# Attention scores for the row maxima as two half-height products, norms merged by pairs of heads, casts moved to ScalarE

## The chip, the cores and the metric

One core of a Trainium2 chip runs the whole program in one launch. The metric is the device time of the program in microseconds; smaller is better. The engines named in the profile are PE (TensorE, its matmuls), PEld (its weight loads), DVE (VectorE), ACT (ScalarE), POOL (GpSimd) and SP (SyncE, which issues most DMAs).

## The reference

The program is an attention block, a routing of tokens to experts and two feed-forward layers. Only the first part is touched by the change. It has B = 4, H = 8, S = 576 and D = 64:

```python
scores = scale * np.matmul(q, k.transpose(0, 1, 3, 2))
scores = np.where(causal, -1000000000.0, scores)
scores = scores - scores.max(-1, keepdims=True)
a = np.exp(scores)
a /= a.sum(-1, keepdims=True) + 1e-09
local = np.matmul(a, v)
...
q_p = phi(q)
mem_ret = np.einsum('bhsd,bhde->bhse', q_p, M_prev)
mem_norm = np.einsum('bhsd,bhd->bhs', q_p, z_prev)[..., None] + 1e-06
mem_out = mem_ret / mem_norm
return (g * mem_out + (1 - g) * local).astype(np.float32)
```

After it each token goes to one of 8 experts by a greedy pass over all gate values with a capacity of 288, through `relu(x @ w1) @ w2` of its expert, and through `max(x @ w1, x @ w2, x @ w3) @ w_out`.

## The kernel before

The heads are worked on in 16 pairs. The scores of a head are computed twice. The first time rows of q are the partitions (`s`, line L509 for the four full blocks of 128 rows, L511 for the last 64 rows of both heads), and VectorE takes each row's maximum from PSUM (L528, an operation and a read of its accumulator). The maxima are turned by a product with the identity (L562), copied by ScalarE and written by a small DMA into an extra row of `QL`. The second time keys are the partitions (`t`, L629 and L630, four groups for each head), with the maximum already subtracted by that extra row; ScalarE takes the exponential into `PT` (L640), GpSimd cuts the triangle off (L658), and fifteen products with V for each head (`av`, L675) add up the output and the row sum. The norm (L693, L696, L700, L704, all on VectorE) divides and adds to `x`, which already holds the memory part (`mem`, L724; L748).

Precision comes from splitting float32 into two float32r parts. `Kr` and `Qr` hold each head's 64 rows of k and q twice, in partitions 0 to 63 and 64 to 127. `QX` is the rounded q in both halves; `KX` is the rounded k in both halves, from which the lower half is then replaced by the rest k - KX. One product over 128 partitions therefore gives q times (rounded k + rest). `KB` and `QL` carry the other rest. The three casts of a head (`KX`, `QX`, `KB`, all recorded at the helper line L312) may go to ScalarE or VectorE, whichever a planner finds sooner free; the rests (recorded at L84) go to GpSimd. The products with V and those of L724 and L407 are plain float32 and appear as two records each.

What sets the order: every piece of work is a task with a key, a cost for each engine and the ring of buffers that it needs. `Plan.run` simulates the engines with those costs and writes all instructions out in the order in which it started them. Keys and costs of `PRIO`, `act`, `dve` and the numbers at each `add` thus set the order on all five engines; each engine runs its list strictly in order. The rings that matter here are `s` with 3 PSUM banks, `t` with 2, `av` with 2 (one for each head of a pair) and `mem` with 1. To keep PSUM for the fourth, 64-wide score group of a head, that group is written into unused columns of the head's `av` bank:

```python
bt = Buf(R["t"]) if gi < 3 else r.bav[i]
```

While the first data is loading, TensorE runs 32 products of a constant (`warm`, L790) in pairs over 64 partitions each; their result is not used. 24 conversions of the second layer's weights (L869 on ScalarE, L873, L876, L879 on VectorE) fill gaps of the attention. The attention ends when the last gate values are in `L`; then the routing begins on VectorE and TensorE.

Of the kernel before, what the change touches and what calls it, by code (L numbers as in the profile page):

```python
# [22 lines left out]
F32 = mybir.dt.float32  # L23
# [32 lines left out]
BUFS = {'Kr': 2, 'Qr': 2, 'QN': 2, 'MZ': 2, 'V': 3, 'VT': 2, 'phi': 2, 'ph': 1, 'KX': 6, 'QX': 5, 'QL': 2, 'KB': 4, 'QJ': 3, 'nm': 3, 'nmr': 1, 'n9': 1, 'PT': 2, 's': 3, 't': 2, 'r5': 2, 'tmp': 3, 'rm': 2, 'x': 2, 'm2raw': 2, 'm2a': 1, 'm2b': 1, 'x2': 2}  # L56
OFFK = (0, 576, 1024, 1344, 1536)
ACTX = 0
PRIO = {'load': -12, 'phi': 2.0, 'min2': ['ACT'], 'prep': 7.5, 'cpe': ['ACT', 'DVE'], 'sube': ['POOL'], 'S': -71.0, 'J4': -2.0, 'R': -78.0, 'E': 29.0, 'N': -37.5, 'T': -3.0, 'A': 18.5, 'M': -60.0, 'rowe': ['ACT'], 'maske': ['POOL'], 'norm': 0.5, 'xadd': ['DVE'], 'mem': [0, 9], 'gate': 45.5, 'G': -13.0, 'gev': ['ACT'], 'm2': [15.0, 4.6, 25.0]}
# [7 lines left out]
NROW, COLD, NLAT = 1, 6000, 3000  # L67
# [64 lines left out]
class Plan:  # L132
# [28 lines left out]
    def run(self):  # L161
# [7 lines left out]
        while len(order) < len(self.tasks):  # L169
            best, hold, cands = None, {}, []  # L170
            for t in ready:
                blocked, users = False, []
                for b in t.new:
                    k = len(b.ring.made) - b.ring.n
                    if k >= 0:
                        users += b.ring.made[k].users
                if any(u.end is None for u in users) or not all(b.made for b in t.use):
                    continue
                for e, c in t.engs.items():
                    if e == "PE" and now < self.cold:  # L180
                        c *= 2
                    at = 0
                    for d in t.deps:
                        at = max(at, d.end + (LAT[d.eng][e] + d.slack * (d.eng != e) if d.lat is None else d.lat))
                    for u in users:
                        at = max(at, u.end + (0 if u.eng == e else LAT[u.eng][e]))
                    st = max(at, free.get(e, 0), now)
                    cands.append((t, e, c, st))
# [57 lines left out]
def attention(g, tc, ctx, consts, beta, qT, kT, qN, v1, vT, mz, mT, wg, xd, L, m2):  # L246
# [20 lines left out]
    AV = [ps.tile([128, 512], F32, name=f"av{i}") for i in range(2)]  # L267
# [4 lines left out]

    def av3(t):
        return t[:, :NJ * C].rearrange("p (j c) -> p j c", j=NJ)
# [30 lines left out]
    def act(n, psum=False):  # L305
        return 22 + 0.89 * n if psum else 60 + 0.89 * n
# [37 lines left out]
    def pair(p):  # L344
# [92 lines left out]
        r.tphi = add(kp + .2, {"DVE": dve(S)}, phi3, [a], use=[b_["ph"], b_["phi"], b_["QN"]])  # L437
# [10 lines left out]
        def head(i):  # L448
# [13 lines left out]
            def sk(e):  # L462
                sub(nc, e, r.KX[i][64:], r.Kr[64:, i], r.KX[i][64:].bitcast(F32))
# [12 lines left out]
            sb = {x: {"POOL": 1390, "DVE": dve(S)}[x] for x in W["sube"]}  # L476
            if not p:
                cp, sb = {"ACT": act(S), "DVE": dve(S, False)}, {"POOL": 1390, "DVE": dve(S)}
# [12 lines left out]
    def maxes(r, p):  # L491
# [5 lines left out]
        def piece(key, heads, j, a, z, first, last, dep):  # L497
# [6 lines left out]
            for x, i in enumerate(heads):  # L504
                def fS(e, i=i, x=x):
                    if x == 0:
                        o.s = ps.tile([128, 512], F32, name="s", bufs=BUFS["s"])
                    if j < 4:
                        nc.tensor.matmul(o.s[:, :z - a], r.QX[i][:, 128 * j:128 * j + 128], r.KX[i][:, a:z], start=True, stop=True)  # L509
                    else:  # L510
                        nc.tensor.matmul(o.s[:, :z - a], u.QJ[:, i], r.KX[i][:, a:z], start=x == 0, stop=x == len(heads) - 1)  # L511

                ts.append(add(key + 5 * heads[-1] + W["S"], {"PE": mm(z - a)}, fS, r.th[i] + ts[-1:] + u.prev + (tj[i:i + 1] if j == 4 else []),
                              new=[bs] if x == 0 else [],
                              use=[r.bh[i]["KX"], r.bh[i]["QX"]] + [bs] * x + ([bj] if j == 4 else [])))

            def fR(e):
# [15 lines left out]
            ttr.append(add(key + 5 * heads[-1] + W["R"], {"DVE": max(dve(z - a), 196)}, fR, ts + dep, new=[bnm] if new else [],  # L533
# [12 lines left out]
        each = []  # L546
        for i in range(2):
            e0 = len(ttr)
            for j in range(4):
                piece(n + j, (i,), j, 0, 128 * j + 128, True, True, ttr[-1:])  # L550
            if p < NROW:
                t = piece(n + 4, (i,), 4, 0, 512, True, False, ttr[-1:])
                piece(n + 4, (i,), 4, 512, S, False, True, t)
            each.append(ttr[e0:])
# [49 lines left out]
    def unit(r, p, i):  # L604
# [14 lines left out]
        for gi, gr in enumerate(groups):  # L619
            o = K()  # L620
            bt = Buf(R["t"]) if gi < 3 else r.bav[i]

            def fT(e, gr=gr, o=o, gi=gi):
                o.t = ps.tile([128, 512], F32, name="t", bufs=BUFS["t"]) if gi < 3 else AV[h % 2][:, 448:512]
# [23 lines left out]
        for gi, (kb, cnt, st) in enumerate(((0, 2, 576), (2, 2, 320), (4, 1, 64))):  # L648
# [12 lines left out]
            c = {"DVE": dve(cnt * m), "POOL": 40 + 1.25 * cnt * m}  # L661
# [3 lines left out]
        for j in range(NJ):  # L665
            m = rows(j)

            def fA(e, j=j, m=m):

                av = AV[h % 2][:, j * C:j * C + CA]  # L670
                for kb in range(j + 1):
# [3 lines left out]
                    nc.tensor.matmul(av[:m], u.PT[:kr, o:o + m], r.Vw[:kr, c:c + CA],  # L675
                                     start=(kb == 0), stop=(kb == j))

            out.append(add(n1 + W["A"] + .1 * j, {"PE": (222, 444, 666, 888, 700)[j]}, fA,
                           mk[:1] + (fill if p == 0 else []) + (ex[1:2] if j else []) + (mk[1:2] if j > 1 else []) + (mk[2:] if j > 3 else []) + [r.tV] + out[-1:],
                           use=[bP, r.b["V"], r.bav[i]]))  # L680
        return out

    def norm(r, p, i, deps, mems):
        b, pp = divmod(p, H // 2)
        h = 2 * pp + i
        n = r.n + 5 * i + 4 + W["norm"]
        av = av3(AV[h % 2])
# [3 lines left out]
        def f1(e):  # L691
            u.r5 = tile("r5", [128, NJ])
            V.tensor_scalar(u.r5, av[:, :, 72], 1.0e-9, g.c1[:, h:h + 1], op0=OP.add, op1=OP.mult)  # L693
# [4 lines left out]
        def f3(e):  # L698
            u.tmp = tile("tmp", [128, NJ, 72])
            V.tensor_mul(u.tmp, av[:, :, :72], u.r5[:, :, None].to_broadcast([128, NJ, 72]))  # L700

        def f4(e):
            for x, c0, c1 in ((x2s[b].t[:, :, h], 0, 64), (xs[b][:, :, h], 64, 72)):
                vg(e).tensor_add(x, x, u.tmp[:, :, c0:c1])  # L704

        t = add(n, {"DVE": 130}, f1, deps + [cdone], new=[br], use=[r.bav[i]])
        t = add(n + .1, {"DVE": 100}, f2, [t], use=[br])
        t = add(n + .2, {"DVE": dve(360)}, f3, [t], new=[bt], use=[br, r.bav[i]])
        c = {"POOL": 1020, "DVE": dve(320) + 90}
        return add(n + .3, {x: c[x] for x in (W["xadd"] if p < NP - 1 else ("POOL", "DVE"))}, f4, [t] + mems, use=[bt, r.bx, r.bx2])  # L710

    def mem(r, p, part):
# [39 lines left out]
        t = add(n + .1, {"DVE": 75}, f1, [t, cdone], new=[br], use=[bm])  # L752
        t = add(n + .2, {"DVE": 80}, f2, [t], use=[br])
        return add(n + .3, {"DVE": dve(144 * k) + 70}, f3, [t] + ([firsts[b]] if b in firsts else []),
# [67 lines left out]
    for p in range(NP):  # L822
# [24 lines left out]
    def conv(k):  # L847
# [36 lines left out]
        t2 = add(n + W["m2"][2], {"DVE": 335}, f2, [t0], new=[bb], use=[br])  # L884
        t3 = add(n + W["m2"][2] + .1, {"DVE": 602}, f3, [t1, t2], use=[ba, bb])
        add(n + W["m2"][2] + .2, {"DVE": 602}, f4, [t3], use=[br, bb])
# [689 lines left out]
```

## Time and profile before

| | us |
|---|---|
| median of three runs | 941.97 (934.69, 941.97, 942.91) |
| the profiled execution's own time | 938.56 |
| its span, first to last instruction | 936.8 |
| TensorE busy | 863.9 (92%) |
| VectorE busy | 570.9 (61%) |
| GpSimd busy | 433.6 (46%) |
| ScalarE busy | 316.5 (34%) |

Shares over the whole span mix stages. The attention fills the first 297 us or so, the routing of the first expert some 60 us after it, and the experts the rest. A matmul's end is modelled, so that a TensorE that shows as busy can still be slowed by weight loads; how far apart two products start says more than how long each is shown. A float32 product is two records.

### The profile page before, as it was taken

To read this page: it belongs to the slowest core of one execution; us is meant where nothing else is said; L and a number is where in the kernel's file an instruction comes from. 1 tells how busy PE (TensorE), PEld (TensorE's weight loads), DVE (VectorE), ACT (ScalarE), POOL (GpSimd) and SP (SyncE) were. 2 spreads that over 40 slices of the span, in tenths; PEclk is the share of its full clock that TensorE was granted. 3 is DMA by queue.
4 is the path that set the end of the run, shared out by engine and by line. 5 is a ranking of instruction groups with operands and counts; after the bars stand their busy time and mean duration, and the time that the engine had idled before them with its cause. 6 is when DMAs were issued, how large, how long until landed. Compare 5 with 4: busy or idle time off the path is not lost.

```text
span 936.8 us, 17494 instructions
## 1 busy us (share of the span) xinstructions
PE 863.9 (92%) x6493; PEld 788.0 (84%) x6493; DVE 570.9 (61%) x1708; ACT 316.5 (34%) x683; POOL 433.6 (46%) x665
## 2 busy tenths in 40 slices
PE   8999999999997467999989998999999999979997
PEld 5888888888886357989979988989998998979996
DVE  5699999997756864842682683484376386123121
ACT  3445555553334032223124133224223224322211
POOL 1758777677421396344064155136208326730301
PEclk9699999999998569999999999999999999989999
DMA  7456776854201122231042032024014114340000
GB/s 282 164 200 201 252 256 218 281 162 133 94 18 52 54 62 91 72 112 46 2 138 91 2 115 95 21 79 138 23 47 146 38 52 154 116 91 23 24 1 34
DMA packets 37601, 97.86 MB, mean 104 GB/s; under 512 B 9620, under 2 KB 9740, under 8 KB 37516
## 3 DMA queue, kind: packets, MB, share of 16 engines
q1 hardware_dynamic: 34240, 87.24, 28.8%
q0 software_dynamic: 2976, 9.44, 3.0%
q8 instruction: 51, 0.84, 0.4%
q14 instruction: 34, 0.28, 0.1%
q10 hardware_dynamic: 300, 0.07, 0.0%
HBM read 87.22 MB, written 9.45 MB: 103 GB/s over the span
## 4 chain that ended last, share of the span: by engine, by line
PE 61%; DVE 11%; POOL 10%; issue 8%; DMA 8%; ACT 2%; SPq 0%; POOLq 0%; ACTq 0%; DVEq 0%
PE av L675 10%; PE w L1323 7%; PE w L1325 7%; PE w L1324 7%; DMA wraw<-in_wr 5%; PE acc L1325 4%; PE acc L1323 4%; PE acc L1324 4%; POOL ml L84 4%; POOL wlo L84 3%; PE s L509 3%; PE t L629 2%; PE mem L724 2%; PE t L630 2%; PE mem L407 2%
## 5 line engine op out<-in xcount | busy, mean ns | idle before, releaser
L84 POOL TENSOR_TENSOR wlo<-wraw,whi 128x256 fp32r<-128x256 f32 x224 | 167.6, 783 | 253.2 <-ACT whi L1289 251.1
L1323 PE MATMUL w<-yh,mh 128*128 128x288 f32 x576 | 175.1, 304 | 4.8 <-ACT mt L1425 4.8
L1324 PE MATMUL w<-yl,mh 128*128 128x288 f32 x576 | 171.7, 298 | 0.1
L1325 PE MATMUL w<-yh,ml 128*128 128x288 f32 x576 | 171.1, 297 | 0.0
L675 PE MATMUL av<-V,PT 128*128 128x112 f32 (+2 forms) x960 | 130.7, 275 | 0.0
L675 PEld LDWEIGHTS av<-V,PT 128*128 128x128 f32 (+2 forms) x960 | 114.9, 174 | 13.7 <-issue 4.6
L1323 PEld LDWEIGHTS w<-yh,mh 128*128 128x128 f32 x576 | 109.9, 191 | 8.0 <-ACT mt L1425 5.0
L1324 PEld LDWEIGHTS w<-yl,mh 128*128 128x128 f32 x576 | 109.9, 191 | 3.4 <-DVE yl L1229 0.3
L1325 PEld LDWEIGHTS w<-yh,ml 128*128 128x128 f32 x576 | 110.1, 191 | 0.0
L1227 DVE SCALAR_TENSOR_TENSOR hl<-w,hh 128x288 fp32r<-128x288 f32 x64 | 28.8, 456 | 132.3 <-ACT hh L1221 132.3
L1427 DVE TENSOR_TENSOR mt<-w,mt 128x288 f32<-128x288 f32 x96 | 43.5, 453 | 102.9 <-PE w L1325 84.0
L1289 ACT CAST whi<-wraw 128x1024 fp32r<-128x1024 f32 x64 | 67.2, 1049 | 114.9 <-DMA wraw<-in_wr 89.9
L528 DVE CUSTOM_DVE_ANT_0 junk<-s,mask 128x256 bf16<-128x256 f32 (+4 forms) x145 | 72.8, 505 | 23.6 <-PE s L509 19.8
L1325 PE MATMUL w<-xhi,wlo 128*128 128x288 f32 x256 | 77.7, 304 | 8.1 <-DVE wlo L78 7.5
L640 ACT ACTIVATE PT<-t 128x512 f32<-128x512 f32 x96 | 54.5, 594 | 78.7 <-PE av L675 48.7
L1323 PE MATMUL w<-xhi,whi 128*128 128x288 f32 x256 | 78.0, 305 | 1.1 <-ACT whi L1289 1.1
L1324 PE MATMUL acc<-hl,whi 128*128 128x288 f32 x256 | 76.8, 300 | 0.8 <-DVE hl L1227 0.8
L1324 PE MATMUL w<-xlo,whi 128*128 128x288 f32 x256 | 77.1, 301 | 0.0
L1323 PE MATMUL acc<-hh,whi 128*128 128x288 f32 x256 | 77.1, 301 | 0.0
L1325 PE MATMUL acc<-hh,wlo 128*128 128x288 f32 x256 | 76.5, 299 | 0.0
L84 POOL TENSOR_TENSOR KX<-Kr,KX 64x192 fp32r<-64x192 f32 x90 | 63.1, 729 | 21.0 <-ACT KX L312 13.8
L658 POOL TENSOR_SCALAR_AFFINE_SELECT PT<-PT 128x256 f32<-128x256 f32 (+1 forms) x96 | 41.2, 440 | 66.7 <-ACT PT L640 61.2
(236 smaller groups left out, 1925.0 us busy)
## 6 DMA issues: line engine op xcount, KB each, us to landing
wraw<-in_wr SPq DMA_DIRECT2D x64, 512.0 KB
Kr<-in_kT SPq DMA_DIRECT2D x15, 576.0 KB
Qr<-in_qT SPq DMA_DIRECT2D x15, 576.0 KB
V<-in_v SPq DMA_DIRECT2D x16, 384.5 KB
m2raw<-in_m2w SPq DMA_DIRECT2D x12, 512.0 KB
QN<-in_qN SPq DMA_DIRECT2D x16, 288.0 KB
VT<-in_vT SPq DMA_DIRECT2D x16, 288.0 KB
xd<-x SPq DMA_DIRECT2D x16, 256.0 KB
```

The costliest lines, as they stand in the source:

```text
L84: u = nc.gpsimd.tensor_sub(o[:, c], a[:, c], b[:, c])
L509: nc.tensor.matmul(o.s[:, :z - a], r.QX[i][:, 128 * j:128 * j + 128], r.KX[i][:, a:z], start=True, stop=True)
L528: V.tensor_tensor_reduce(out=junk[ps_, :z - a], in0=o.s[ps_, :z - a], in1=mask[ps_, k:k + z - a], scale=-0.125, scalar=init, op0=OP.add, o ...
L640: A.activation(u.PT[:kr, at0:at0 + wd], o.t[:kr, :wd], AF.Exp, scale=0.125)
L658: G.affine_select(v, v, pattern=[[1, m]] if cnt == 1 else [[0, 2], [1, m]], compare_op=OP.is_ge, fill=0.0, base=0, channel_multiplier=-1)
L675: nc.tensor.matmul(av[:m], u.PT[:kr, o:o + m], r.Vw[:kr, c:c + CA], start=(kb == 0), stop=(kb == j))
L1227: V.scalar_tensor_tensor(lo(), src(), 0.0, hi().bitcast(F32), op0=OP.max, op1=OP.subtract)
L1289: A.copy(x.W[fb][0], x.RAW[fb])
L1323: nc.tensor.matmul(o, wh, rh, start=start, stop=False)
L1324: nc.tensor.matmul(o, wh, rl, start=False, stop=False)
L1325: nc.tensor.matmul(o, wl, rh, start=False, stop=stop)
L1427: V.tensor_max(q.mt, o.pt[:, :T], q.mt)
```

## The change

1. `fS` for the four full blocks: both heads' products are issued back to back, head 0 from partitions 0 to 63 of `KX` and `QX`, head 1 from partitions 64 to 127, each into its own bank of `s`. They use the rounded k alone. For that `sk` writes head 1's rest into the upper half of `KX`, so that its rounded k stays in the lower one. The reductions (`reduce`, split off from `piece`) stay one for each head and block. The last 64 rows (L511) are as before.
2. `norm` is called once for a pair, over both `av` banks, which are now one tile `AVP`. A head's first product with V therefore takes a bank that the norm of the whole pair before releases. The last block's product with V writes 73 columns in place of 112.
3. The 64-wide score group goes into a bank of the `t` ring.
4. `cpe` is ScalarE alone, but for the first pair.
5. Keys and costs of the planner are other numbers, its check of free buffers counts two new buffers of one ring in one task, and it doubles TensorE's costs in its first 25,000 ns in place of 6,000. `xadd` is on VectorE for the last pair too.

```diff
-BUFS = {... 'tmp': 3, ...}
+BUFS = {... 'tmp': 2, ...}
...
-PRIO = {'load': -12, 'phi': 2.0, ... 'cpe': ['ACT', 'DVE'], 'sube': ['POOL'], 'S': -71.0, 'J4': -2.0, 'R': -78.0, 'E': 29.0, 'N': -37.5, 'T': -3.0, 'A': 18.5, 'M': -60.0, ... 'norm': 0.5, ...}
+PRIO = {'load': -22, 'phi': -18.0, ... 'cpe': ['ACT'], 'sube': ['POOL'], 'S': -51.0, 'J4': -2.0, 'R': -96.0, 'E': 29.0, 'N': -47.5, 'T': -41.0, 'A': 40.5, 'M': 10.0, ... 'norm': -9.5, ...}
...
-NROW, COLD, NLAT = 1, 6000, 3000
+NROW, COLD, NLAT = 1, 25000, 3000
...
-    AV = [ps.tile([128, 512], F32, name=f"av{i}") for i in range(2)]
+    AVP = ps.tile([128, 2, 512], F32, name="av")
+    AV = [AVP[:, i] for i in range(2)]
...
     def act(n, psum=False):
-        return 22 + 0.89 * n if psum else 60 + 0.89 * n
+        return 135 + 0.89 * n if psum else 155 + 0.89 * n
...
             def sk(e):
-                sub(nc, e, r.KX[i][64:], r.Kr[64:, i], r.KX[i][64:].bitcast(F32))
+                q = slice(64 - 64 * i, 128 - 64 * i)
+                sub(nc, e, r.KX[i][q], r.Kr[q, i], r.KX[i][q].bitcast(F32))
...
-        each = []
+
+        each = [[], []]
+        for j in range(4):
+            bs = [Buf(R["s"]) for _ in range(2)]
+            os = [K(), K()]
+            z = 128 * j + 128
+
+            def fS(e, j=j, z=z, os=os):
+                for i in range(2):
+                    os[i].s = ps.tile([128, 512], F32, name="s", bufs=BUFS["s"])
+                for i in range(2):
+                    q = slice(64 * i, 64 * i + 64)
+                    nc.tensor.matmul(os[i].s[:, :z], r.QX[i][q, 128 * j:z], r.KX[i][q, :z], start=True, stop=True)
+
+            t = add(n + j + W["S"], {"PE": mm(z) + 60}, fS, r.th[0][:2] + r.th[1][:2] + u.prev, new=bs,
+                    use=[r.bh[i][x] for i in range(2) for x in ("KX", "QX")])
+            for i in range(2):
+                each[i] += reduce(n + j + .5 * i, (i,), j, 0, z, True, True, ttr[-1:], os[i], slice(0, 128), bs[i], [t])
         for i in range(2):
-            e0 = len(ttr)
-            for j in range(4):
-                piece(n + j, (i,), j, 0, 128 * j + 128, True, True, ttr[-1:])
...
-            bt = Buf(R["t"]) if gi < 3 else r.bav[i]
+            bt = Buf(R["t"])
...
-                av = AV[h % 2][:, j * C:j * C + CA]
+                w = CA if j < 4 else C
+                av = AV[h % 2][:, j * C:j * C + w]
...
-    def norm(r, p, i, deps, mems):
+    def norm(r, p, deps, mems):
...
         def f3(e):
-            u.tmp = tile("tmp", [128, NJ, 72])
-            V.tensor_mul(u.tmp, av[:, :, :72], u.r5[:, :, None].to_broadcast([128, NJ, 72]))
+            u.tmp = tile("tmp", [128, NJ, 2, 72])
+            V.tensor_mul(u.tmp, av[:, :, :, :72], u.r5[:, :, :, None].to_broadcast([128, NJ, 2, 72]))
...
-        for i in range(2):
-            last = unit(r, p, i)
-            nm.append(norm(r, p, i, last, [m0, m1]))
+        last = unit(r, p, 0) + unit(r, p, 1)
+        r.avs = [r.bav[0], r.bav[1]]
+        nm.append(norm(r, p, last, [m0, m1]))
```

**The order on TensorE.** Before, in the second and third pair, the score products for the maxima (`s<-KX,QX`) stand one by one between products with V (`av`) and the gate's products (`mem<-wb,VT`); the next head's products with V follow on the other bank.

```order
L675 MATMUL av_109<-V,PT 128x112 x4
L509 MATMUL s<-KX,QX 128x128 [waits DVE_49,Pool_49]
L675 MATMUL av_109<-V,PT 64x112 x5
L509 MATMUL s<-KX,QX 128x256 [waits DVE_49,Pool_49]
L407 MATMUL mem<-wb,VT 128x96 [waits DMAHW4_49,DVE_49]
L407 MATMUL mem<-wb,VT 128x96 x3
L407 MATMUL mem<-wb,VT 64x96
L509 MATMUL s<-KX,QX 128x384
L675 MATMUL av_110<-V,PT 128x112
L509 MATMUL s<-KX,QX 128x512 [waits DVE_49,Pool_49]
```

After, at the boundary between the third and the fourth pair, they stand in twos (`x2`, or two rows where the second waits for something else), and the new pair's first product with V, the last row, waits for VectorE (the norm of the pair before) and GpSimd.

```order
L557 MATMUL s<-KX,QX 128x128 [waits DVE_49] x2
L574 MATMUL s<-ident,nm 9x128 [waits DVE_49]
L641 MATMUL t<-QX,KX 128x320 [waits Activation_49]
L642 MATMUL t<-QL,KB_127 128x320
L641 MATMUL t<-QX,KX 128x192
L642 MATMUL t<-QL,KB_127 128x192
L405 MATMUL mem<-wb,VT 128x96 [waits DVE_49]
L405 MATMUL mem<-wb,VT 128x96 x3
L405 MATMUL mem<-wb,VT 64x96
L641 MATMUL t<-QX,KX 64x64 [waits Activation_49]
L642 MATMUL t<-QL,KB_127 64x64
L557 MATMUL s<-KX,QX 128x256 [waits DVE_49]
L557 MATMUL s<-KX,QX 128x256 [waits Activation_49]
L688 MATMUL av<-V,PT 128x112 [waits DVE_49,Pool_49]
```

In all, the score products for the maxima moved together by twos, and the `t` groups of the next heads stand between the last product with V of a pair and the first of the next.

**The order on VectorE.** Before, in the first pair, head 0's norm begins with `r<-av,c` and releases the bank with `tmp<-av,r`; a row maximum, a cast, a reciprocal and a weight conversion stand between.

```order
L693 TENSOR_SCALAR r_596<-av_109,c_120 128x5 [waits PE_49]
L528 ISA junk,nm<-s,mask 128x256 [waits DVE_49,PE_49]
L528 ISA nm 128x1
L312 CAST KX<-Kr 128x576 [waits DMAHW7_49]
L696 RECIPROCAL r_596<-r_596 128x5 [waits DVE_49]
L876 SCALAR_TENSOR_TENSOR m2b<-m2a,m2b 128x512 [waits Activation_49]
L700 TENSOR_TENSOR tmp<-av_109,r_596 128x360 [waits DVE_49]
```

After, the norm at the boundary between the third and the fourth pair: the same two ends, over 10 and 720 elements, and between them the memory part's `x<-mem,rm` and two row maxima.

```order
L707 SCALAR_TENSOR_TENSOR r_1130<-av,c_119 128x10 [waits PE_49]
L762 TENSOR_TENSOR x_467<-mem,rm 128x3x128 [waits DVE_49]
L762 TENSOR_TENSOR x<-mem,rm 128x3x16
L527 ISA junk,nm<-s,mask 128x128 [waits PE_49]
L527 ISA nm 128x1
L710 RECIPROCAL r_1130<-r_1130 128x10 [waits DVE_49]
L527 ISA junk,nm<-s,mask 128x128 [waits PE_49]
L527 ISA nm 128x1
L714 TENSOR_TENSOR tmp<-av,r_1130 128x720 [waits DVE_49]
```

The norms of two heads became one, the cast of `KX` left this engine, and row maxima that wait for TensorE still stand inside the norm.

## Rows read from the trace of the kernel before

**Rows 1.** Busy time by engine in stretches (microseconds, instructions), granted clock, DMA share, GB/s

```profile
core 0: us, PE busy (x) PEld busy (x) DVE busy (x) ACT busy (x) POOL busy (x), PEclk, DMA share, GB/s
...
28.00:45.00 17.00, 16.54 (x64) 14.68 (x65) 10.70 (x39) 8.10 (x19) 13.41 (x24) 0.51 0.39 132
...
60.00:200.00 140.00, 137.44 (x1000) 119.29 (x1000) 134.31 (x430) 75.13 (x160) 106.14 (x161) 1.00 0.72 236
200.00:280.00 80.00, 76.67 (x562) 66.78 (x562) 57.07 (x196) 31.98 (x69) 41.66 (x110) 1.00 0.29 91
...
```

**Rows 2.** Waits of TensorE from 60 to 280 us, longest in total first

```profile
PE s L562 <- DVE nm L528: 3.4, 4, 1.0
...
```

**Rows 3.** Timeline of TensorE's products, 240.2 to 243.1 us: start, duration, instruction

```profile
240.29 0.42 PE L509 MATMUL s<-KX,QX 128*128 128x384 f32 x1
240.65 1.31 PE L675 MATMUL av<-V,PT 128*64 128x112 f32 x10
241.89 0.50 PE L509 MATMUL s<-KX,QX 128*128 128x512 f32 x1
242.23 0.37 PE L675 MATMUL av<-V,PT 128*128 128x112 f32 x2
242.37 0.48 PE L511 MATMUL s<-KX,qj 128*128 128x512 f32 x1
242.68 0.59 PE L675 MATMUL av<-V,PT 128*128 128x112 f32 x4
```

**Rows 4.** Timeline of TensorE's products, 2 to 12.4 us

```profile
2.48 3.00 PE L790 MATMUL av<-warm 64*128 64x384 f32 x16 [2.48 <-DVE av L270]
...
7.47 0.58 PE L509 MATMUL s<-KX,QX 128*128 128x256 f32 x1
7.98 0.69 PE L790 MATMUL av<-warm 64*128 64x384 f32 x2
8.60 0.69 PE L509 MATMUL s<-KX,QX 128*128 128x384 f32 x1
...
```

**Rows 5.** Timeline of TensorE's products, 233 to 252 us, 64-wide scores

```profile
236.40 0.19 PE L629 MATMUL av<-QX,KX 128*64 128x64 f32 x1
236.44 0.22 PE L630 MATMUL av<-QL,KB 65*64 65x64 f32 x1
236.49 0.90 PE L675 MATMUL av<-V,PT 128*128 128x112 f32 x6
```

**Rows 6.** Groups of VectorE by form, 0 to 305 us: busy us, mean ns | idle before

```profile
L704 DVE TENSOR_TENSOR x<-x,tmp 128x320 f32<-128x320 f32 x32 | 21.5, 672 | 0.3
...
L700 DVE TENSOR_TENSOR tmp<-av,r 128x360 f32<-128x360 f32 x32 | 16.9, 527 | 0.4
...
L704 DVE TENSOR_TENSOR x<-x,tmp 128x40 f32<-128x40 f32 x32 | 11.6, 362 | 0.0
L312 DVE CAST KB<-Kr 64x576 fp32r<-64x576 f32 x19 | 11.3, 595 | 0.5 <-PE av L630 0.5
L528 DVE CUSTOM_DVE_ANT_0 junk<-s,mask 128x128 bf16<-128x128 f32 x32 | 9.0, 282 | 3.3 <-PE s L509 3.3
...
L312 DVE CAST QX<-Qr 128x576 fp32r<-128x576 f32 x13 | 7.1, 556 | 0.0
L693 DVE TENSOR_SCALAR r<-av,c 128x5 f32<-128x5 f32 x32 | 7.1, 221 | 15.5 <-PE av L675 13.4 <-ACT mh L1200 2.0
L696 DVE RECIPROCAL r<-r 128x5 f32<-128x5 f32 x32 | 5.9, 184 | 0.2
...
```

**Rows 7.** Groups of ScalarE by form, 0 to 305 us

```profile
L312 ACT CAST KX<-Kr 128x576 fp32r<-128x576 f32 x19 | 12.5, 662 | 0.0
...
```

**Rows 8.** Timeline of TensorE's products, 24.3 to 28.5 us

```profile
27.38 0.42 PE L590 MATMUL t<-identr,nmr 128*1 128x128 f32 x4 [1.53 <-DVE nmr L584]
```

More of the change, by code (lines that the diff above doesn't have):

```diff
@@ L171, in run @@
             for t in ready:
-                blocked, users = False, []
-                for b in t.new:
-                    k = len(b.ring.made) - b.ring.n
+                users = []
+                for y, b in enumerate(t.new):
+                    k = len(b.ring.made) - b.ring.n + sum(q.ring is b.ring for q in t.new[:y])
                     if k >= 0:
@@ L436, in pair @@
         a = add(kp + .1, {"ACT": act(S)}, phi2, [a], use=[b_["ph"]])
[L437 removed]
+        r.tphi = add(kp + .2, {"DVE": dve(S) + 140}, phi3, [a], use=[b_["ph"], b_["phi"], b_["QN"]])
         def scale(e):
@@ L507, in fS @@
                         o.s = ps.tile([128, 512], F32, name="s", bufs=BUFS["s"])
[L508 to L511, printed above, removed]
+                    nc.tensor.matmul(o.s[:, :z - a], u.QJ[:, i], r.KX[i][:, a:z], start=x == 0, stop=x == len(heads) - 1)
                 ts.append(add(key + 5 * heads[-1] + W["S"], {"PE": mm(z - a)}, fS, r.th[i] + ts[-1:] + u.prev + (tj[i:i + 1] if j == 4 else []),
@@ L515, in piece, with reduce @@
                               use=[r.bh[i]["KX"], r.bh[i]["QX"]] + [bs] * x + ([bj] if j == 4 else [])))
+            return reduce(key, heads, j, a, z, first, last, dep, o, ps_, bs, ts)
+        def reduce(key, heads, j, a, z, first, last, dep, o, ps_, bs, ts):
             def fR(e):
@@ L532, in piece @@
             new = not ttr
-            ttr.append(add(key + 5 * heads[-1] + W["R"], {"DVE": max(dve(z - a), 196)}, fR, ts + dep, new=[bnm] if new else [],
+            ttr.append(add(key + 5 * heads[-1] + W["R"], {"DVE": 235 + 1.02 * (z - a)}, fR, ts + dep, new=[bnm] if new else [],
                            use=[bs] + ([] if new else [bnm])))
@@ L620, in unit @@
             o = K()
-            bt = Buf(R["t"]) if gi < 3 else r.bav[i]
+            bt = Buf(R["t"])
             def fT(e, gr=gr, o=o, gi=gi):
-                o.t = ps.tile([128, 512], F32, name="t", bufs=BUFS["t"]) if gi < 3 else AV[h % 2][:, 448:512]
+                o.t = ps.tile([128, 512], F32, name="t", bufs=BUFS["t"])
                 c = 0
@@ L698, in f3 @@
         def f3(e):
-            u.tmp = tile("tmp", [128, NJ, 72])
-            V.tensor_mul(u.tmp, av[:, :, :72], u.r5[:, :, None].to_broadcast([128, NJ, 72]))
+            u.tmp = tile("tmp", [128, NJ, 2, 72])
+            V.tensor_mul(u.tmp, av[:, :, :, :72], u.r5[:, :, :, None].to_broadcast([128, NJ, 2, 72]))
         def f4(e):
             for x, c0, c1 in ((x2s[b].t[:, :, h], 0, 64), (xs[b][:, :, h], 64, 72)):
[L704 to L710, printed above, removed]
+                vg(e).tensor_add(x, x, u.tmp[:, :, :, c0:c1])
+        t = add(n, {"DVE": 214}, f1, deps + [cdone], new=[br], use=r.avs)
+        t = add(n + .1, {"DVE": 180}, f2, [t], use=[br])
+        t = add(n + .2, {"DVE": dve(720) + 60}, f3, [t], new=[bt], use=[br] + r.avs)
+        c = {"POOL": 2040, "DVE": 1250}
+        return add(n + .3, {x: c[x] for x in W["xadd"]}, f4, [t] + mems, use=[bt, r.bx, r.bx2])
     def mem(r, p, part):
```

43 lines of the change are left out of this document (20 added, 23 removed).

## Prediction

> **What bounds the kernel now.** I read the busy time by stretches first, then TensorE's waits, then its timeline. The attention ends near 297 us; the order behind it is unchanged, so what the change is worth is how much earlier that end comes. From 60 to 200 us TensorE is busy for 137.4 of 140 us at the full clock, VectorE for 134.3, GpSimd for 106, ScalarE for 75 [rows 1]. Two engines look full, and which one is the bound decides everything. The list of TensorE's waits answers: in 220 us it waited for VectorE in four waits of 3.4 us together that are worth naming [rows 2], and its products otherwise start at spacings that repeat. So TensorE is the bound, VectorE is merely as busy, and work taken off VectorE gives back little more than those 3.4 us. I therefore price the change on TensorE.
>
> **Prices on TensorE.** All from the timeline. A product with V over 128 columns of weights and 112 moving columns takes 0.11 us for each of its two records. A 512-column score product between two such takes 0.45 - 2 x 0.11 = 0.23 us (242.23 to 242.68) [rows 3], that is 512 columns at 2.4 GHz (0.213) and about 0.02 to 0.03 us. With 0.03 for each, the four blocks of a head are 1280 columns, 0.53 + 0.12 = 0.65 us, 1.30 for a pair.
>
> What does a product over 64 partitions cost among others over 128? At the start, with the engine at 1.2 GHz, the rows show it. Sixteen of the constant products, issued by twos over the two halves, take 3.0 us, 0.32 to 0.37 for two of 384 columns, so the two halves do run side by side (384 columns at 1.2 GHz are 0.32). But two of them alone between score products take from 7.98 to 8.60, 0.62 us, and the 256-column score product before them 0.51 where its columns take 0.21 [rows 4]: 0.30 us goes at each change between the two forms. At full clock I have the plain float32 products with 64 columns of weights, the last two of them over 64 partitions. From 240.29 to 242.23 stand a 384-column score product, ten such records and a 512-column one [rows 3]. Without changes that would be 0.19 + 10 x 0.095 + 0.24 = 1.38 (0.093 are 2 x 112 columns at 2.4 GHz); it took 1.94. Three changes cost 0.56, 0.19 each. Half of the 0.30 at half the clock is 0.15. These are the ends; I take 0.16, nearer to the lower, since a start is shown a little early behind a faster stream. The 64-wide float32r score groups pay nothing of the kind (starts 0.04 to 0.05 apart [rows 5]), so narrow weights alone are no change of form there.
>
> The Trainium skill, page TensorEngine Tiling (Array Packing), section Key Properties, says that a change of tiling mode, as against a change of tile, drains TensorE, while tiles of one mode work independently. The start rows agree on both, with 0.30 us for a change; the page gives no price.
>
> **The change part by part.**
> 1. *Score products by twos.* The columns of one of two products are saved: 0.65 us for a pair. Behind the first pair's products with V, the order holds 57 such twos: 57 x 0.163 = -9.3 us. The same order has 228 changes of form against 138 (counted over rows of half height and of narrow float32). 90 x 0.16 = +14.4 us, between +13.5 and +17. If weights could be loaded across the change, it would be 0: that is a rival.
> 2. *73 columns in place of 112.* Each of 30 blocks has ten records, 2 x 39 columns fewer at 2.4 GHz, 0.0325 us each: 0.31 us allowing for the two that follow a change. 30 x 0.31 = -9.3. It holds only if 64 columns of weights load faster than 0.06 us; three starts 0.04 and 0.05 apart say so [rows 5]. The other end is 0, if the 0.095 us are weight loading.
> 3. *Maxima and the small product that waits for them* (L562). Its wait for VectorE is 3.4 us [rows 2]. It now stands two to three microseconds of TensorE work behind the last row maximum, and VectorE loses work: -3, between 0 and -3.4.
> 4. *Casts.* 18 of `KB` at 0.595, 12 of `QX` at 0.556 and 12 of `KX` leave VectorE, about 23 us [rows 6], and cost ScalarE 42 x 0.66 = 28 us [rows 7]. ScalarE goes from 75 of 140 us to some 91, and its small DMA issues come on top. Hidden on both sides by TensorE; 0. If that cover failed, exponentials queued behind a cast of 0.66 us would hold the two `t` banks and TensorE with them: I keep +4 for it.
> 5. *Merged norm.* For two heads now 2 x (0.22 + 0.18 + 0.53 + 0.67 + 0.36) = 3.9 us [rows 6]. Merged, two small ones of about 0.2, one multiply of 0.9 to 1.05 and the two adds of 1.0 and 0.4: 2.7, so some 19 us less on VectorE, again behind TensorE. New is the wait: the next pair's first product with V needs both banks, so the release comes 0.2 + 0.2 + 1.0 and the notice, some 1.6 us after the last product of the pair, and with the memory part and two row maxima standing between, 2.6 to 3 us. Behind the waiting product all of TensorE's queue stands. Ahead of it, after the boundary shown in the order, are four to five `t` groups, a gate step of ten records and two score twos: 0.5 + 1.2 + 0.6 + 0.9 and more, about 3.7 us. It is covered by 0.7 us there. In the last three pairs no score products for maxima are left, the cover is about 1.7 us, and I put +0.6 for each. The end of the last norm is 2.7 against 1.9: +0.8. Sum +2.6, between +1 and the rival below.
> 6. *The `t` bank for the 64-wide group.* Four groups for a head instead of three go through two banks; ScalarE's 0.21 us for it is short. 0, kept within item 4's bound.
> 7. *Start.* Both heads' q and k must be there before the first score product, and the early changes of form cost 0.30 each; against this, the casts that stood ahead of the maxima on VectorE are gone, and with them a wait of 1.5 us at 27.4 us [rows 8]. From 28 to 45 us the granted clock is 0.51, that is 1.2 GHz, right behind that wait and with TensorE busy for 16.5 of 17 us [rows 1]. If the clock did not fall, up to half of it, 8 us, would be won; if the start comes later, 4 us lost. I take -2.
>
> Sum: -9.3 + 14.4 - 9.3 - 3 + 2.6 - 2 = -6.6. From the profiled execution's 938.56 us (span 936.8, 1.8 around it) this gives **932**. The median of the three runs, 941.97, lies 3.4 us above that execution and the lowest run 3.9 below, so the sum is as good as its base to some 4 us.
>
> **The rivals.**
> *The change of form is hidden* (the halves run side by side and nothing else is paid). For it: the half products' weights need other partitions' space only, and the constant products overlap fully. Against it: both of the two directions cost 0.30 at the start. Time: 932 - 14.4 = 918, own range 914 to 923. The page's section Theoretical Speedup, up to twofold for a contraction of 64 or less, points this way.
> *The merged norm comes late* (slower). The row maxima that stand inside the norm wait for score twos, and these wait for two of three `s` banks, which earlier row maxima must release: each waits for the other in turn. A maximum is 0.28 + 0.08 us [rows 6]; two such rounds and the memory part in line delay the release by 1 to 2 us. It decides from the 0.7 us of cover on: at 2 us late, 15 boundaries x 1.3 = +19, so 951, own range 943 to 957. For it: nothing on TensorE between can pass the waiting product. Against it: VectorE has 40 us less to do.
> *The narrow products save nothing*, being bound by weight loading: 932 + 9.3 = 941, own range 937 to 946.
> *The clock stays full from 25 us on*: 932 - 6 = 926.
>
> **How the numbers follow.** Chances: the forecast 0.45 (own range 925 to 939), hidden changes 0.22, late norm 0.13, no saving from narrow products 0.12, the clock 0.08. One per cent, 9.4 us, is about what a measurement of this kernel can tell from no change; against 942, faster lies below 932.5 and slower above 951.4. Faster: half of the forecast, hidden changes, most of the clock, 0.48. Slower: half of the late norm and what I have not seen, 0.12. Same 0.40. The range reaches from the middle of the hidden changes to the middle of the late norm's lower half, **917 to 948**; cases of both signs are in it.
>
> **What would show it.** The timeline after: two half-height score products with equal starts, and 0.15 to 0.19 us more than their columns before and behind them (right), or the next weight load starting under them (first rival). The ten-record blocks at 0.92 in place of 1.24 us. TensorE still busy over 95% from 60 to 200 us while VectorE falls below 85%. The wait of the small product L562 gone from the list of waits; a wait of `av` for `tmp` in its place would be the late norm. ScalarE's exponentials as what `t` waits for would show item 4 wrong. The granted clock between 25 and 45 us shows item 7. I am wrong in kind if TensorE's work for a pair turns out not to be what sets the end.

## The result, and the profile after

The changed kernel takes 931.89 us (median of 12 runs, 926.36 to 934.79) against 940.18 us (median of 12 runs, 934.69 to 948.06): ratio 0.9903, interval 0.9876 to 0.9930. Its profiled execution took 933.35 us (span 931.6). The forecast of 932 is met, but not by its own sum.

I split each profiled execution at the start of the last product with V. Before, that is at 294.4 us, with 642.4 us from there to the end; after, 281.5 and 650.2. So the attention became 12.9 us shorter, twice the 6.6 us forecast, and 7.8 us came back behind it, where only the end of the last norm was changed. The busy time by stretches, answering [rows 1]:

```profile
28.00:45.00 17.00, 17.00 (x114) 13.90 (x112) 9.85 (x40) 7.57 (x17) 9.29 (x17) 1.00 0.29 97
60.00:200.00 140.00, 137.50 (x1006) 114.57 (x1005) 107.07 (x346) 82.36 (x172) 91.95 (x167) 0.99 0.64 205
200.00:280.00 80.00, 79.16 (x604) 67.68 (x605) 57.69 (x179) 42.97 (x89) 43.94 (x105) 1.00 0.40 131
```

VectorE falls from 134 to 107 us of 140 and TensorE stays at 98%. The stretch from 28 to 45 us, at 0.51 before, is at full clock from 32.7 us on (see below). Only part of VectorE's 27 us are casts and norms: the three steps of the weight conversions (L887, L890, L893) take 26.5 us there, 45.9 before, because the new order puts more of them behind 200 us; the casts that left took 12.5 (that is more than 27 in all, and more of the other work falls into the stretch). TensorE's waits from 60 to 280 us, answering [rows 2] (total, times, longest):

```profile
PE t L641 <- ACT PT L652: 1.8, 4, 0.8
PE av L688 <- issue: 0.5, 1, 0.5
PE s L557 <- DVE nm L527: 0.4, 1, 0.4
...
```

The wait of the small product is gone, and none of `av` for `tmp` has come. TensorE's timeline, answering [rows 3, 5], with one two (s, x2) between `t` groups, and a ten-record block:

```profile
97.93 0.40 PE L642 MATMUL t<-QL,KB 65*128 65x512 f32 x1
98.26 0.38 PE L557 MATMUL s<-KX,QX 64*128 64x256 f32 x2
98.57 0.30 PE L641 MATMUL t<-QX,KX 128*128 128x64 f32 x1
...
98.82 0.45 PE L641 MATMUL t<-QX,KX 128*128 128x448 f32 x1
...
106.41 0.99 PE L688 MATMUL av<-V,PT 128*64 128x73 f32 x10
107.33 0.30 PE L641 MATMUL t<-QX,KX 128*128 128x64 f32 x1
```

The block takes 0.92 us to the next start (1.24 before, both as forecast). The two stands 0.33 us behind a product of 0.21 us of columns, and 0.31 us ahead of the next, where its columns are 0.11. The start, answering [rows 4, 8]; a value in brackets is a wait:

```profile
6.95 1.02 PE L557 MATMUL s<-KX,QX 64*128 64x128 f32 x2 [0.71 <-DVE QX L310]
...
9.65 0.58 PE L557 MATMUL s<-KX,QX 64*128 64x256 f32 x1 [0.93 <-DVE nm L527]
...
31.45 0.77 PE L641 MATMUL t<-QX,KX 128*128 128x512 f32 x1
32.02 0.63 PE L642 MATMUL t<-QL,KB 65*128 65x512 f32 x1
...
45.51 0.39 PE L641 MATMUL t<-QX,KX 128*128 128x512 f32 x1
45.74 0.40 PE L642 MATMUL t<-QL,KB 65*128 65x512 f32 x1
```

The same product is 0.57 us from the next start at 31.45 and 0.23 us at 45.51: TensorE ran at 1.2 GHz up to 32.7 us, where its clock records begin, and at 2.4 GHz from there. (The views print 1.00 also where no record is.) Before, it was at full clock from 24.2 to 27.6, then at half for 17.1 us.

VectorE's groups (first five lines, answering [rows 6]) and ScalarE's casts (answering [rows 7]):

```profile
L718 DVE TENSOR_TENSOR x<-x,tmp 128x640 f32<-128x640 f32 x16 | 15.4, 961 | 0.0
L714 DVE TENSOR_TENSOR tmp<-av,r 128x720 f32<-128x720 f32 x16 | 14.4, 901 | 0.1
L718 DVE TENSOR_TENSOR x<-x,tmp 128x80 f32<-128x80 f32 x16 | 7.6, 477 | 0.0
L710 DVE RECIPROCAL r<-r 128x10 f32<-128x10 f32 x16 | 3.4, 212 | 0.1
L707 DVE SCALAR_TENSOR_TENSOR r<-av,c 128x10 f32<-128x10 f32 x16 | 2.7, 168 | 9.4 <-PE av L688 9.3
```

```profile
L310 ACT CAST KB<-Kr 64x576 fp32r<-64x576 f32 x31 | 20.7, 668 | 10.7 <-PE t L642 7.1 <-DMA QL<-n 1.5 <-PE s L557 1.3
...
L310 ACT CAST KX<-Kr 128x576 fp32r<-128x576 f32 x31 | 20.5, 665 | 6.8 <-DMA Kr<-in_kT 4.9 <-issue 1.8
```

A merged norm is 0.96 + 0.90 + 0.48 + 0.21 + 0.17 = 2.72 us (2.7 forecast), and 31 of each kind of cast are on ScalarE, 19 `KX` before.

### The profile page after: what moved, and what is told of

It reads as the page before. It is cut to its first block, busy times and chain, and to the rows that moved or that the text cites. A ratio compares the mean times of both kernels' runs of the same rounds, so it can differ in the third digit from the quotient of the medians.

```text
span 931.6 us, 17277 instructions
## 1 busy us (share of the span) xinstructions
PE 857.7 (92%) x6493; PEld 777.3 (83%) x6493; DVE 538.5 (58%) x1598; ACT 336.6 (36%) x709; POOL 422.9 (45%) x669
## 4 chain that ended last, share of the span: by engine, by line
PE 64%; POOL 10%; DVE 8%; issue 8%; DMA 7%; ACT 2%; ACTq 0%; SPq 0%; POOLq 0%; DVEq 0%
PE av L688 11%; PE w L1337 7%; PE w L1339 7%; PE w L1338 7%; DMA wraw<-in_wr 6%; POOL wlo L84 5%; PE acc L1339 4%; PE acc L1337 4%; PE acc L1338 4%; PE t L641 4%; POOL ml L84 4%; PE t L642 3%; PE mem L738 3%; PE s L557 2%; PE mem L405 2%
## 5 line engine op out<-in xcount | busy, mean ns | idle before, releaser
L688 PE MATMUL av<-V,PT 128*128 128x112 f32 (+2 forms) x960 | 119.8, 268 | 1.0 <-issue 0.5
L688 PEld LDWEIGHTS av<-V,PT 128*128 128x128 f32 (+2 forms) x960 | 107.0, 175 | 14.6 <-issue 6.1
L652 ACT ACTIVATE PT<-t 128x512 f32<-128x512 f32 (+1 forms) x128 | 61.6, 499 | 64.3 <-PE av L688 30.0
L670 POOL TENSOR_SCALAR_AFFINE_SELECT PT<-PT 128x256 f32<-128x256 f32 (+1 forms) x96 | 41.3, 436 | 79.7 <-ACT PT L652 79.1
L641 PE MATMUL t<-QX,KX 128*128 128x512 f32 (+2 forms) x192 | 65.6, 356 | 1.9 <-ACT PT L652 1.8
```

The lines of the kernel that those rows point to most:

```text
L641: nc.tensor.matmul(o.t[:kr, c:c + z - a], r.KX[i][:, ks], r.QX[i][:, a:z], start=True, stop=False)
L652: A.activation(u.PT[:kr, at0:at0 + wd], o.t[:kr, :wd], AF.Exp, scale=0.125)
L670: G.affine_select(v, v, pattern=[[1, m]] if cnt == 1 else [[0, 2], [1, m]], compare_op=OP.is_ge, fill=0.0, base=0, channel_multiplier=-1)
```

## The experiments

All ratios are to the kernel before. "End" is the start of the last product with V in the profiled execution.

| kernel | end, us | from there to the end | ratio (interval) |
|---|---|---|---|
| before | 294.4 | 642.4 | 1 |
| changed | 281.5; again 280.9 | 650.2; 646.8 | 0.9903 (0.9876 to 0.9930) |
| e1 full-height scores | 274.1; again 275.0 | 654.1; 651.0 | 0.9844 (0.9791 to 0.9896) |
| e2 112 columns | 288.4 | 644.1 | 0.9982 (0.9946 to 1.0018) |
| e3 order and casts alone | 281.6 | 642.1 | 0.9894 (0.9855 to 0.9934) |
| e4 73 columns alone | 290.8 | 642.3 | 0.9944 (0.9901 to 0.9988) |
| e5 pause filled | 292.8 | 643.5 | 0.9994 (0.9960 to 1.0027) |
| e6 casts alone | 282.4 | 646.3 | 0.9895 (0.9858 to 0.9932) |
| e7 numbers alone | 295.4 | 643.7 | 0.9899 (0.9838 to 0.9960) |
| e8 order, casts, 73 columns | 271.8 | 647.2 | 0.9731 (0.9674 to 0.9789) |
| e9 73 columns everywhere | 271.9 | 645.1 | 0.9784 (0.9738 to 0.9829) |
| e10 casts, 73 columns | 284.5 | 643.7 | 0.9867 (0.9802 to 0.9931) |

**e1: the twos undone in the changed kernel.**

```diff
-nc.tensor.matmul(os[i].s[:, :z], r.QX[i][q, 128 * j:z], r.KX[i][q, :z], ...)
+nc.tensor.matmul(os[i].s[:, :z], r.QX[i][:, 128 * j:z], r.KX[i][:, :z], ...)
```

> The changed kernel with one thing undone: the score products for the row maxima of blocks 0 to 3 are again two products over all 128 partitions, one after the other, at the very places in the order where the twos stood. By the forecast's prices (columns saved 9.3 us, 90 more changes of form at 0.16 us, 14.4 us) this is 5 us faster than the changed kernel, about 927 us or 0.986 of the kernel before. By what the starts in the changed kernel's trace show (a way into the half-height form and back costs about 0.20 us more than two starts in one form, some 3.4 more ways for a pair, 0.67 us, against 0.62 us of columns saved) it is within 1 us of the changed kernel: 931 to 933, and a pair in the middle takes 16.0 to 16.3 us as there. If the change of form were hidden, it would be 9 us slower, 941.

The end comes 7.3 us earlier (274.15 against 281.45), and 5.8 in the second execution of each. The two numbers differ partly by the start: the first execution of e1 alone has 3.4 us at full clock from 6.5 us on. The same stretch as above, in e1:

```profile
94.85 0.39 PE L642 MATMUL t<-QL,KB 65*128 65x512 f32 x1
95.08 0.40 PE L557 MATMUL s<-KX,QX 128*128 128x256 f32 x2
95.32 0.19 PE L641 MATMUL t<-QX,KX 128*128 128x64 f32 x1
...
95.46 0.45 PE L641 MATMUL t<-QX,KX 128*128 128x448 f32 x1
```

From the 512-column product to the 448-column one these are 0.61 us, against 0.89 with the two: it saves 0.11 us of columns and costs 0.28 net. So the forecast's price is right in kind and a little low, and my later reading (no difference), which had put a way in and back at 0.20 us above two starts in one form, is wrong.

**e2: 112 columns again in the changed kernel.** Edit: `w = CA if j < 4 else C` to `w = CA`.

> The changed kernel with one thing undone: the products with V for the fifth block stream 112 columns again in place of 73, same order. If these ten-record blocks are bound by their columns, as forecast, each goes from 0.92 back to about 1.24 us: 32 x 0.32 = 10 us slower than the changed kernel, about 942. If they are bound by weight loading: no difference, 932.

The blocks are 1.24 us again, and the end moves by +6.9 us, less than the 10 expected. The changed kernel loses 1.7 us to 3.4 us at half clock at 169 us, which this one has not; with these, 8.6. In these blocks columns bind, not weights.

**e3: the planner's numbers and the casts alone, in the kernel before.**

```diff
-PRIO = {'load': -12, 'phi': 2.0, ... 'cpe': ['ACT', 'DVE'], ... 'S': -71.0, ... 'T': -3.0, 'A': 18.5, ...}
+PRIO = {'load': -22, 'phi': -18.0, ... 'cpe': ['ACT'], ... 'S': -51.0, ... 'T': -41.0, 'A': 40.5, ...}
...
-NROW, COLD, NLAT = 1, 6000, 3000
+NROW, COLD, NLAT = 1, 25000, 3000
```

> The kernel before with the planner's numbers of the changed one (priorities, costs, the span in which it takes TensorE as slow) and its rule that the casts go to ScalarE, and with none of the other edits: full-height scores, norms by heads, 112 columns. Theory: the changed kernel's gain at the start (its second pair of heads ends 11.3 us earlier, about 4.3 us of that by work put off) comes from the order and the casts, which leave no wait before 33 us, so that the clock does not fall back. Then the second pair ends 7 to 11 us before 74.2 us, the granted clock is 1.00 from 33 to 45 us, and the time is 930 to 935; a pair in the middle still takes 16.3 to 16.6. Rival: the gain at the start is that of the twos themselves, two heads' maxima in the time of one: then the second pair ends within 3 us of 74.2 us and the time is 938 to 942.

Its second pair ends at 64.8 us (74.2 before) and its attention at 281.6: with none of the other edits it has all of the changed kernel's gain. Only part of that is the start. TensorE's waits over its whole attention, then those of the kernel before (without the row of [rows 2], 3.4 us):

```profile
PE av L790 <- DVE av L270: 2.5, 1, 2.5
PE s L509 <- DVE QX L312: 1.4, 1, 1.4
PE av L675 <- ACT PT L640: 0.5, 2, 0.2
PE av L629 <- DVE tmp L700: 0.4, 1, 0.4
```

```profile
...
PE t L590 <- DVE nmr L584: 1.5, 1, 1.5
PE t L629 <- ACT PT L640: 1.2, 1, 1.2
PE s L509 <- DVE KX L78: 1.0, 1, 1.0
PE s L509 <- POOL PT L658: 0.9, 1, 0.9
PE t L592 <- ACT QL L312: 0.7, 1, 0.7
PE s L511 <- DVE nm L528: 0.6, 2, 0.3
PE s L509 <- DVE nm L528: 0.2, 1, 0.2
```

Behind the first 2.5 us, which both have, that is 2.3 us against 9.5. TensorE is at half clock until 32.5 us and full from then on, against 24.2 + 17.1 = 41.3 us: 8.8 us less, worth about 4.4 (half of it). Waits and clock make 11.6 of the 12.8 us.

**e5: the pause before the clock's fall filled, in the kernel before.**

```diff
+                for _ in range(6 * i):
+                    nc.tensor.matmul(u.ta, warm[:, :128], warm, start=True, stop=True)
                 for j in range(4):
                     nc.tensor.matmul(u.ta[0:1, 128 * j:128 * j + 128], ...)
```

> The kernel before with six more products of 512 columns (their result is overwritten) put in front of the four small ones whose wait of 1.53 us for VectorE ended at 27.38 us, so that TensorE is busy through that wait. If the clock fell at 27.6 us because of this pause, it now stays at 1.00 from 28 to 45 us and up to 8 us are won: 932 to 936. If something else made it fall, it is at 0.51 there as before, and the time is that of the kernel before or up to 1 us more.

```profile
28.00:45.00 17.00, 15.14 (x99) 12.57 (x97) 12.72 (x50) 9.26 (x21) 12.78 (x23) 1.00 0.31 108
```

```profile
26.95 2.91 PE L590 MATMUL t<-warm 128*128 128x512 f32 x6
...
31.07 0.68 PE L509 MATMUL s<-KX,QX 128*128 128x128 f32 x3
...
42.97 0.33 PE L509 MATMUL s<-KX,QX 128*128 128x128 f32 x1 [1.19 <-POOL KX L84]
```

The clock is full from 30.2 us on and does not fall. It also rose later than before (24.2 us), and 30.2 us at half clock stand against 41.3. From the three score products to the next pair's first one are 11.9 us here, 17.6 before (28.60 to 46.19). But the end moves by 1.6 us only and the ratio is 1: the added products took 2.5 us, and what TensorE gained beyond that it then waited (the 1.19 us, 1.8 for `nm`). This one execution fits the theory that the pause brings the fall but does not prove it, since the rise moved too, and the wait of 1.19 us was followed by none. A full clock alone buys little while other engines are late.

**e4: 73 columns alone, in the kernel before.** Edit: `w = CA if j < 4 else C`, with `w` in place of `CA` in the product.

> The kernel before with the fifth block's products with V at 73 columns in place of 112 and nothing else; the order stays. By the blocks' own prices (1.24 us before, 0.92 after, 32 blocks) 10 us faster, about 929. By the reverse in the changed kernel, where putting the 112 columns back moved the end of the attention by 6.9 us: about 933. If VectorE holds TensorE up in this order, so that TensorE's saved time turns into waits: 936 to 940.

The blocks are at 0.92 us, worth 9.8, and the end moves by 3.6. In its list of waits stand

```profile
PE t L629 <- ACT PT L640: 3.6, 5, 1.5
PE s L562 <- DVE nm L528: 3.1, 3, 1.0
```

and the clock falls for 3.4 us at 86 and for 6.8 us at 172 us. In the old order part of TensorE's savings turns into waits and half clock. But it is not VectorE that makes it wait longer, as the expectation had it: `nm` stands at 3.4 before and 3.1 here, the exponentials at 1.2 and 3.6. Ahead of the longest of these, ScalarE waits for a load of q (`in_qT`), and the exponential stands in line behind that cast:

```profile
84.66 0.24 ACT L312 CAST qj<-Qr 128x64 fp32r<-128x64 f32 x1 [2.05 <-DMA Qr<-in_qT]
...
85.45 0.30 PE L629 MATMUL t<-QX,KX 128*128 128x64 f32 x1 [1.48 <-ACT PT L640]
```

**e6 and e7: the casts alone (`'cpe': ['ACT']`), and the other numbers alone (e3 with `'cpe': ['ACT', 'DVE']`).**

> The kernel before with the rule that the casts of the heads after the first pair go to ScalarE, and nothing else; the planner places the work anew with its old numbers. If it is the casts that took TensorE's waits away (VectorE's load from 60 to 200 us falls from 134 us of 140 to some 111), the attention ends some 7 us or more before 294.4 us and the time is 930 to 935. Rival: the priorities and costs do it: the attention ends at 291 us or later, 937 to 942.

> The kernel before with all the planner's numbers of the changed one, but with the casts free to go to either engine, as before. If the priorities and costs do it, the attention ends near 281.6 us as with the casts moved too, 928 to 933. If the casts do it: it ends at 290 us or later, 936 to 941.

e6 ends at 282.4, so one entry gives 12.0 of the 12.9 us. e7's profiled execution ends at 295.4, but it ran at half clock for 17 us behind waits (100 and 202 us), worth 8.5, and was one of the longest of its runs (940.8; five of eight took 928.8 to 930.9). Its ratio is as good as e6's. So by time either half suffices, and together they are not worth more; the one trace of e7 does not show it (without the first 2.5 us its waits are 7.0 us, 9.5 before), and its short runs were not profiled. Both relieve VectorE from 60 to 200 us (121 and 114 us, 112 in e3), but not by the same work. In e6 the casts left it. In e7 it still has 47 of the 96 casts (45 before); there the conversions of weights, one step of which is shown from before and from e7, moved behind 200 us (25.5 us in place of 45.9 for the three steps):

```profile
L876 DVE SCALAR_TENSOR_TENSOR m2b<-m2a,m2b 128x512 int32<-128x512 int32 x23 | 18.8, 816 | 0.3
```

```profile
L876 DVE SCALAR_TENSOR_TENSOR m2b<-m2a,m2b 128x512 int32<-128x512 int32 x12 | 9.1, 758 | 0.0
```

Each of these edits also lets the planner place all work anew; a lighter VectorE and a better order are not told apart.

**e8 and e9: e3 with 73 columns, in the fifth block and everywhere.**

> The kernel before with the planner's numbers and the casts of the changed one (its attention ended at 281.6 us, ratio 0.989) and with the 73 columns: full-height scores and norms by heads remain. If the columns are worth 6.9 us here too, the attention ends at 274.7 us and the ratio is about 0.982. Against the changed kernel with full-height scores (274.1 us), which differs from this one by the merged norms and the second bank of `t` alone and by the order that follows from them, it shows what those cost: as forecast (2.6 us) this one would end at 271.5 us; at no cost, at 274.

> The kernel before with the planner's numbers and casts of the changed one and 73 columns in the fifth block (ratio 0.973, attention ends at 271.8 us), and now 73 columns in all products with V, 112 nowhere. In the other four blocks a record has 128 columns of weights and takes 0.114 us where its 2 x 112 columns are 0.093. If columns bound it, 800 records lose up to 0.033 us each, 26 us; if it is the loading of 128 columns of weights (0.11 us), as I now think, the end of the attention moves by less than 5 us. It tells whether the forecast's rule for the fifth block, columns and not weights, holds only for narrow weights.

e8 ends at 271.8: with few waits (2.4 us behind the first 2.5) the columns are worth 9.8 us, the full price. It is the best kernel found. By its time it gains 15 us on e3, by the trace 10; the intervals are wide enough for both. In e9 the end does not move. The row of 18 records, first e9, then e8:

```profile
92.81 2.12 PE L676 MATMUL av<-V,PT 128*128 128x73 f32 x18
```

```profile
92.96 2.16 PE L676 MATMUL av<-V,PT 128*128 128x112 f32 x18
```

The median spacing is 0.112 us at 73 columns and at 112. With 128 columns of weights the moving columns do not bind; that leaves the loading of weights.

**e10: casts and 73 columns.**

> The kernel before with two things: the casts to ScalarE (alone: attention ends at 282.4 us, ratio 0.990) and 73 columns in the fifth block (worth 9.8 us of the attention where TensorE has no waits, 3.6 us where VectorE holds it up), the planner's other numbers as before. If the casts freed TensorE, the columns are worth their full price here: the attention ends at 272 to 274 us, ratio 0.977 to 0.982. If VectorE (121 of 140 us here) still holds TensorE up: 278 us or later, 0.985 or more.

The end, 284.5, and the ratio, 0.9867, lie in the second range, but not for its reason: behind the first 2.5 us TensorE waits 1.9 us for VectorE. Part of it are waits for exponentials and what followed them:

```profile
PE t L629 <- ACT PT L640: 3.1, 3, 1.5
```

```profile
98.40:108.60 10.20, 10.20 (x42) 8.82 (x42) 5.30 (x16) 5.16 (x11) 3.74 (x7) 0.50 0.60 204
```

Three falls of the clock, 20.4 us in all, are worth 10.2 us; by this estimate it would have ended at 274.3 without them, as expected of freed casts. Ahead of the two longest waits (1.54 and 1.34 us) ScalarE had waited 2.56 and 2.11 us for the load of q, as in e4. e8, which has the planner's other numbers too, has no such wait; which of the numbers does it was not tested.

**Two profiles again.**

> The changed kernel as it is, profiled once more. From the last product with V to the end its first profiled execution took 650.2 us, the kernel before 642.4, and ten executions of variants with the same work there between 642.1 and 654.1. If that spread is chance (a load of expert weights that lands 3 us late, stretches of 3.4 us at half the clock behind short waits), this part takes 642 to 648 us now. If the changed kernel's end of the attention itself causes it, 649 to 654 again. In the attention, the 3.4 us at half the clock at 169 us come again if the wait for exponentials ahead of them does.

> The changed kernel with full-height score products, profiled once more. Its first execution ended the attention at 274.1 us, 2.3 us behind the variant without merged norms (271.8), with 3.4 us at half the clock at 163 us, worth 1.7 us, that the other had not. If the merged norms cost next to nothing, an execution without that stretch ends near 272.4; at their forecast price of 2.6 us it ends near 274.4. The part behind the attention took 654.1 us: 642 to 648 now if that was chance, 649 or more if not.

The two executions took 929.42 and 927.78 us. The ends repeat within 1 us, and so does the fall of the clock near 165 us behind waits for exponentials. Behind the attention the answers differ: the changed kernel's 646.8 lies in the range given to chance, e1's 651.0 in the other. The full-height kernel ends at 275.0 with the fall, 273.3 without its 1.7 us, midway between the values for norms that cost nothing and norms at their forecast price.

## Why the prediction came out right, point by point

**The sum.** By edits measured one at a time, the attention's 12.9 us are: order and casts -12.8 (e3), 73 columns -9.8 (e8 against e3), twos +6.6 (e1, mean of two executions of each), merged norms with the second `t` bank and the order that follows +2.8 (e1 at 274.6 against e8). That is -13.2. The forecast had -5 for what e3 holds, -9.3, +5.1 and +2.6.

- *Item 1, twos:* +5.1 forecast, +6.6 (5.8 to 7.3) measured. With 9.3 us of saved columns, 90 changes cost 15.1 to 16.6 us, 0.17 to 0.18 each, inside the range of 0.15 to 0.19 but above the 0.16 taken; no row shows the reason given for the lower end, that a start is shown early behind a faster stream. The rival of hidden changes is refuted. The Trainium skill, page TensorEngine Tiling (Array Packing), section Theoretical Speedup, gives up to twofold for a contraction of 64; the two products do start together (0.003 to 0.004 us apart in 55 of the 56 recorded behind 33 us), and e1 shows that the way in and out costs more than that here.
- *Item 2, columns:* 9.3 against 9.8; the rival of weight loading is refuted for 64 columns of weights, and e9 leaves it for 128, where 73 and 112 columns take the same 0.112 us.
- *Items 3, 4 and 7, waits, casts, start: the failed step.* "TensorE is the bound, VectorE is merely as busy, and work taken off VectorE gives back little more than those 3.4 us", and with it the zero for the casts. I read one row of the list of waits, from 60 us on. Over the whole attention, behind the first 2.5 us, the list held 9.5 us, 6.7 of them for VectorE. On VectorE ahead of the wait of [rows 8] stand

```profile
24.71 0.72 DVE L312 CAST KB<-Kr 64x576 fp32r<-64x576 f32 x1
...
25.90 0.85 DVE L312 CAST KB<-Kr 64x576 fp32r<-64x576 f32 x1
...
26.68 0.55 DVE L584 CAST nmr<-nm 128x4 fp32r<-128x4 f32 x1
```

  and right behind that wait the clock fell. Order and casts (e3) took away 7.2 us of waits and 4.4 of clock against the 5 forecast; the casts' entry alone (e6) gave 12.0 us. So TensorE was not held up by 3.4 us alone, and the zero for VectorE's relief is refuted. That a lighter VectorE did it, and not the new order, is argued and not shown: in the changed kernel more of VectorE's relief from 60 to 200 us is conversions put off (19.4 us) than casts (12.5), and e7 gains as much time with the casts where they were. Nor was VectorE the only engine that held TensorE up: in e4 the columns gave 3.6 of 9.8 us, and most of the rest went into 2.4 us more of waits for ScalarE's exponentials and 4.1 us more at half clock (worth about 2).
- *Item 4's bound* was partly called on: `t` waits 1.8 us for exponentials, and a fall of the clock for 3.4 us at 169 us follows, 1.7 us more. The two together, 3.5 us, are near the +4 kept, but the cause was another: ahead of the longest wait (0.81 us, until 165.41) no cast stands on ScalarE but three issues of small DMAs and a step of `ph`.
- *Items 5 and 6:* +2.6 forecast, +2.8 measured, but not by the mechanism: no `av` waits for `tmp` (the late norm did not come), and 1.7 of the 2.8 us are that fall of the clock, which e8's order does not have. The wait itself is not shown. The +0.8 for the end of the last norm lies behind the mark used here and was found there: the first product of the routing starts 3.9 us behind the end in the five executions with the merged norm, 3.3 in the nine others.
- *The clock rival* (full from 25 us on) did not come as put; the fall after 28 us went, the rise came 8.5 us later.

**What came back.** The attention gained 12.9 us and the median 8.3. Fourteen executions took 642.1 to 654.1 us from the end on; the changed kernel's were at 650.2 and 646.8, e1's at 654.1 and 651.0. The merged norm's end is 0.6 us of it. For the rest two things can be named, and neither explains it. After the end, the sum of stretches at half clock is 82 and 72 us in the changed kernel, 91 in both of e1, 71 before (10 us of it are 5); but in e8 it is 66, with 647.2 us from the end on. And in all four, TensorE waits for `hh` some 83 us behind the end:

```profile
364.82 0.40 PE L1337 MATMUL acc<-hh,whi 128*128 128x288 f32 x1 [2.29 <-ACT hh L1235]
```

```profile
363.42 1.05 ACT L1303 CAST whi<-wraw 128x1024 fp32r<-128x1024 f32 x1 [4.37 <-DMA wraw<-in_wr]
```

A cast of expert weights ahead of it on ScalarE waits for its load. From that load's issue to the cast are 6.5 to 7.8 us in these four executions, 4.6 before, 5.6 in e3 and 6.1 in e8. But it is 7.7 us in e4 too, where TensorE waits 1.1 us for `hh` and the whole takes 642.3 us all the same. So a late load is no mark of the changed attention. What the 4 to 8 us are, and whether the changed attention or chance brings them, stays open.

So the time was met by errors that cancel, which is luck: 8 us too little for order and casts, 1.5 too little for the price of the twos, and 4 to 8 us that a later part took back.

## What to carry to other kernels

Two engines at 96 and 98% can hold each other up: before a load on the second is priced at zero, add up every wait of the first over the whole stretch, start included, and the time at the lower clock behind each. Test a saving on an engine in the order in which it will run: the same 73 columns were worth 3.6 us in an order where ScalarE stood waiting for loads and 9.8 us in one where it did not. Running two half-height products side by side pays only if the way in and back (about 0.35 us here) is less than the columns saved (0.05 to 0.21), so leave them, or put them next to others of their form, which no run here tried.

## What the runs showed of the hardware

- A short wait of TensorE can be followed by 3.4 to 17 us at half clock and so cost several times its length (e10: 3.1 us of waits for exponentials, two of its three falls right behind them). From 60 us to the end of the attention, all 12 falls in the fourteen executions stand close behind a wait of 0.7 to 1.6 us; but 17 waits of 0.6 to 1.2 us there were followed by none (five of them before). What tells them apart is not shown.
- A product with 128 columns of weights starts every 0.112 us whether 73 or 112 columns stream (e9); with 64 columns of weights, a ten-record block goes from 1.24 to 0.92 us with the columns (e2, e8).
- Two half-height products that start 0.003 us apart can still take longer than two of full height: between full-height products, a two of 256 columns costs 0.28 us more than the two that e1 puts there.
